# Projecting q and k to DRAM beside the kernel transforms, and attention by groups of key blocks with the output projection woven in

## The chip, the cores and the metric

One core of one Trainium2 chip runs the kernel; the other cores are idle. The metric is the device time of one execution in microseconds. A profile (a trace of one execution) counts from its own zero, and its span is about 2 us shorter than the time. Runs are called fast or slow by whether they lie within 1.5% of the fastest of the same kernel; only fast runs are compared.

Names used below: PE is the matmul array, DVE the vector engine, ACT the scalar engine, POOL and SP the two engines that here mostly issue DMA. Each engine works through its own queue in order. The clock of PE is given as the share of full speed that the profile shows as granted; the DMA share is the mean busy share of the 16 DMA engines.

## The reference, cut to what matters

Two branches share one input x (which is also the q of the first), with S = 2048 positions and D = 640 channels, and are mixed by a gate.

```python
def A(q, k, v, shift_k, ssm_k, ssm_D):          # long convolution
    kv = causal_conv4(k, shift_k) * v           # "shift and multiply"
    y  = irfft(rfft(pad(kv)) * rfft(pad(ssm_k)))[:S] + kv * ssm_D
    return q * y

def B(x, wqkv, wo):                             # local dilated attention
    q, k, v = (x @ wqkv) split into 32 heads of 20
    each position sees 8 keys: itself, -2, -4, ... -14 (masked at the start)
    return softmax(q k^T * 20**-0.5) v  @ wo

g = sigmoid(sum(x * gate_w))
return g * A(x, k, v, ...) + (1 - g) * B(x, ...)
```

The kernel computes the Fourier transforms as matmuls against constants (F1b, then G; back through M, then T). In its names `H` is the transform of ssm_k (from `h_lin`, to which D is added), `Up` that of kv, `Cm` the half-inverted product.

## The kernel before

Positions are laid out by parity, so that the dilated window becomes eight neighbours, in 17 blocks of 121 queries and 128 keys, in groups of 4, 4, 3, 3 and 3 blocks. Scores of two heads are two row-tiled matmuls of 31 rows (20 features and 11 mask features). The parts that matter:

```python
# q/k projection: 50 steps of five 128-row matmuls; each head's 20 rows go to SBUF sets by DMA
frag = (dst[r:r + fb - fa, 0:w], stg[fa - f0:fb - f0, 0:w]);  nc.sync.dma_start(*frag)

# attention, by 8 tiles of four heads (all five groups of blocks inside each): 80 halves
for s in range(len(halves)):
    scores(s + 1)                      # PE scores, then one ACT exp per half
    if 6 <= s < 36: advance(qk, 1)     # the last 30 q/k steps woven in
    if s == 20:     load_h()           # h_lin, 8 loads
    if s == 37:     add_D(); hg = h_early()
    if hg is not None and s % 5 != 4: advance(hg, 1)   # kernel transforms woven in
    advance(kvg, 1)                    # DVE's shift-and-multiply chain
    pv(s)

# FFT of kv with the output projection woven in
while advance(fft, 1):
    k += 1
    if k >= 2:  advance(opg, 1)
    if k == 60: load qg (4 DMAs of 640 KB), load bl (4 of 640 KB)       # 32 rows each
T = p2.tile([128, 64, 2, 32], BF, name="T", tag="Am", bufs=2)
nc.sync.dma_start(T[:], cf["T"]...)

# last inverse step: 6 blocks of up to three positions
    for q in range(4):
        nc.vector.tensor_tensor(rq, yv, rq, ALU.mult)                   # yv is in PSUM
    nc.vector.tensor_tensor(reg, reg, bl[:, t0:t0 + m, :], ALU.add)
    for g in range(4):
        (nc.sync, nc.scalar)[g % 2].dma_start(out..., reg...)
```

The softmax here doesn't subtract the row's maximum and nothing guards it: scores larger than these inputs give would overflow.

## Time and profile before

The median of two runs is 356.44 us (355.08 to 357.79); the profiled span is 354.1 us.

| | before |
|---|---|
| PE, DVE, ACT busy share | 72%, 60%, 47% |
| mean granted PE clock | 0.784 |
| DMA moved | 46.37 MB |

No engine is full over the whole span, so the reading has to go by stages, which the prediction does.

### The profile page before, as it was taken

How to read it: one execution, taken by the hardware profiler on the slowest of the kernel's cores; microseconds unless marked ns; L12 is line 12 of the kernel's file. 1: busy time of each engine (PE TensorE's matmuls, PEld its weight loads, DVE VectorE, ACT ScalarE, POOL GpSimd, SP SyncE). 2: the span in 40 equal slices, each digit the busy share in tenths (PEclk: the TensorE clock that was granted, in tenths of full speed). 3: DMA queues.
4: the chain of work that ended last, by engine and by line, in shares of the span. 5: the costliest groups of instructions: out<-in, count | busy, mean ns of one | idle time of the engine just before them, and what ended most of it. 6: DMA issues, size and time to landing. Idle time of an engine off the chain costs nothing. (4 is left out here: it accounts for less than half of the span.)

```text
span 354.1 us, 9846 instructions
## 1 busy us (share of the span) xinstructions
PE 254.6 (72%) x4355; PEld 174.0 (49%) x4355; DVE 211.4 (60%) x295; ACT 165.9 (47%) x239; POOL 41.2 (12%) x67
## 2 busy tenths in 40 slices
PE   2760599958779999857877888898989488660430
PEld 2330355524336655545655655575657477660320
DVE  1400999692836565857776633844574668671595
ACT  3250264525526555634545585756565577531000
POOL 8910023010150000000000000112111000000000
PEclk9995599999659999755555556999999968867555
DMA  7375854974441499761891019217121507999165
GB/s 200 137 241 178 267 151 118 211 199 102 103 84 31 88 168 163 193 191 30 181 213 51 4 27 217 65 41 170 39 54 38 138 4 164 213 213 212 57 149 132
DMA packets 34603, 46.37 MB, mean 131 GB/s; under 512 B 23757, under 2 KB 28572, under 8 KB 33152
## 3 DMA queue, kind: packets, MB, share of 16 engines
q1 hardware_dynamic: 31088, 35.77, 42.9%
q0 software_dynamic: 2896, 8.66, 9.3%
q10 hardware_dynamic: 576, 1.31, 1.6%
q8 instruction: 34, 0.56, 0.7%
q14 instruction: 9, 0.07, 0.1%
HBM read 27.19 MB, written 7.87 MB: 99 GB/s over the span
## 5 line engine op out<-in xcount | busy, mean ns | idle before, releaser
L421 ACT ACTIVATE ET<-sc 128x726 bf16<-128x726 f32 (+1 forms) x80 | 67.1, 858 | 57.8 <-PE sc L418 57.2
L352 PE MATMUL pj<-xT,W 128*128 128x484 bf16 (+3 forms) x250 | 55.9, 368 | 6.2 <-ACT stg L128 4.0
L274 DVE TENSOR_TENSOR pr<-kh,wl 128x2560 bf16<-128x2560 bf16 x16 | 23.0, 1487 | 28.2 <-DMA kh<-in_A_k_dram 23.4
L485 PE MATMUL s<-Am,G 64*128 64x64 bf16 x1280 | 29.2, 206 | 13.9 <-DVE Hs L130 4.1
L352 PEld LDWEIGHTS <-W 128*128 128x128 bf16 x250 | 21.7, 102 | 29.8 <-issue 11.9
L418 PE MATMUL sc<-qb,kb 31*128 31x121 bf16 x544 | 36.0, 260 | 0.6 <-issue 0.6
L485 PEld LDWEIGHTS <-G 64*128 64x128 bf16 x1280 | 26.1, 105 | 17.9 <-issue 12.1
L435 PEld LDWEIGHTS <-ET 128*128 128x128 bf16 x544 | 22.4, 102 | 20.8 <-ACT ET L421 9.3
L618 PE MATMUL op<-wo,oT 128*128 128x128 bf16 (+1 forms) x170 | 27.3, 310 | 4.3 <-ACT oT L128 3.5
L130 DVE CAST stg<-pj 128x484 bf16<-128x484 f32 (+3 forms) x30 | 17.9, 598 | 20.8 <-PE pj L352 16.2
L130 DVE CAST Am<-s 128x512 bf16<-128x512 f32 x36 | 23.4, 686 | 11.5 <-PE s L468 9.9
L309 PE MATMUL psv<-W,xT 128*128 128x128 bf16 (+1 forms) x170 | 27.6, 327 | 2.8 <-DMA W<-in_B_wqkv_dram 2.8
L525 PE MATMUL i<-M,Hw 128*128 128x128 bf16 x160 | 25.6, 253 | 4.9 <-DVE Hw L513 2.6
L525 PE MATMUL i<-M,Hs 128*128 128x128 bf16 x160 | 26.0, 253 | 4.1 <-DVE Hs L512 4.1
L626 POOL DMA_DIRECT2D b_scr<-fin x18 | 9.6, 531 | 161.7 <-DVE fin L624 137.9
L128 ACT CAST Am<-s 128x512 bf16<-128x512 f32 x44 | 23.6, 610 | 6.7 <-PE s L468 4.6
L525 PEld LDWEIGHTS <-Hs 128*128 128x128 bf16 x160 | 22.5, 154 | 7.0 <-DVE Hs L512 4.5
L130 DVE CAST Hs<-s 128x1024 bf16<-128x1024 f32 x15 | 18.4, 1224 | 11.7 <-PE s L485 11.7
L301 PE MATMUL trx<-ident,xS 128*128 128x128 bf16 x80 | 7.9, 265 | 22.6 <-DMA xS<-in_A_q_dram 20.4
L525 PEld LDWEIGHTS <-Hw 128*128 128x128 bf16 x160 | 22.4, 155 | 3.0 <-DVE Hw L513 3.0
L128 ACT CAST Cm<-i 128x1024 bf16<-128x1024 f32 x15 | 15.2, 1012 | 15.9 <-PE i L525 15.7
L309 PEld LDWEIGHTS <-xT 128*128 128x128 bf16 x170 | 14.7, 106 | 15.4 <-issue 7.2
(73 smaller groups left out, 362.5 us busy)
## 6 DMA issues: line engine op xcount, KB each, us to landing
Hw<-Hs SPq DMA_DIRECT2D x10, 512.0 KB
xS<-in_A_q_dram SPq DMA_DIRECT2D x4, 640.0 KB
kv_scr<-pr POOLq DMA_DIRECT2D x4, 640.0 KB, 5.4
h_lin<-in_A_ssm_k_dram SPq DMA_DIRECT2D x8, 320.0 KB
kv<-kv_scr SPq DMA_DIRECT2D x4, 640.0 KB
qg<-in_A_q_dram SPq DMA_DIRECT2D x4, 640.0 KB
bl<-b_scr SPq DMA_DIRECT2D x4, 640.0 KB
W<-in_B_wqkv_dram SPq DMA_DIRECT2D x3, 800.0 KB
```

The costliest lines, as they stand in the source:

```text
L128: self.nc.scalar.copy(dst, src)
L130: self.nc.vector.tensor_copy(dst, src)
L274: nc.vector.tensor_tensor(pr[:, j].rearrange("p (n c) -> p n c", n=4), kh[:, 3 - j:7 - j, :], wl[:, j, :].unsqueeze(1).to_broadcast([128, ...
L309: nc.tensor.matmul(ps[:, n0:n1], lhsT=xT[:, dt, BP * b:BP * b + 128], rhs=W[:, dt, 2, n0:n1], start=(dt == 0), stop=(dt == NDT - 1))
L352: nc.tensor.matmul(ps[:, 0:n], lhsT=W[:, dt, which, 128 * ft:128 * ft + 128], rhs=rhs, start=(dt == 0), stop=(dt == NDT - 1))
L418: nc.tensor.matmul(sc[:, hh, BP * bb:BP * bb + BP], lhsT=kb[r:r + DH + NF, 128 * b:128 * b + 128], rhs=qb[r:r + DH + NF, BP * b:BP * b + B ...
L421: nc.scalar.activation(ETs[s % NET][:, :, 0:nw], sc[:, :, 0:nw], ACT.Exp, scale=SCALE)
L435: nc.tensor.matmul(O[:, sl * 21:sl * 21 + 21], lhsT=ET[:, hh, BP * bb:BP * bb + 128], rhs=VWs[t // 4][:, b, 4 * (t % 4) + 2 * hf + hh, :], ...
L485: nc.tensor.matmul(o, lhsT=st["G"][rows, j, r, :], rhs=Am[rows, 2 * j + r, :, :], start=(r == 0), stop=(r == 1), tile_position=(64 * c, 0) ...
L525: nc.tensor.matmul(o, lhsT=src[:, c, :, :, 8 * oc + il].rearrange("p q j -> p (q j)"), rhs=M[:, k, :], start=(k == 0), stop=(k == 1), skip ...
L618: nc.tensor.matmul(opf[:, n0:n1], lhsT=oT[:, ft, :], rhs=wo[:, ft, n0:n1], start=(ft == 0), stop=(ft == NDT - 1))
L626: nc.gpsimd.dma_start(dst, fin[r0:r0 + n, :])
```

## The change

Its intent, as far as the diff tells: free SBUF and the order of work. q and k are projected at once, beside the transforms of the kernel, and written to DRAM; attention goes group by group over all heads and streams its group back; so a group's output projection can be woven into the next group's attention, and the FFT stands alone. The last step moves PSUM to SBUF by ACT, so that DVE multiplies from SBUF.

```diff
+    q_scr = dpool.tile([D, QW], BF, name="q_scr")
+    k_scr = dpool.tile([D, KW], BF, name="k_scr")
...
-                    frag = (dst[r:r + fb - fa, 0:w], stg[fa - f0:fb - f0, 0:w])
-                        nc.sync.dma_start(*frag)
+                nc.gpsimd.dma_start((q_scr if which == 0 else k_scr)[128 * ft:128 * ft + 128, :], stg[:, 0:w])
...
+    load_h(0); load_G(pC); load_h(1)          # h_lin by group: 40 loads for 8
+    for b in range(12, NB): vproj(b); advance(kvg, 1)
+    for g in range(2, NG): load_h(g)
+    for k in range(50):
+        advance(qk, 1)
+        if k < 10: advance(kvg, 1)
+        if k == 9: nc.vector.tensor_tensor(h_lin[:, :, :, 0], h_lin[:, :, :, 0], Dz..., ALU.add)
+        if k >= 10 and k % 5 != 4: advance(hg, 1)
...
+    def load_bg(gi):                          # one group back: 8 loads of 20 rows
+        for h4 in range(4):
+            r = slice(32 * h4, 32 * h4 + DH)
+            nc.sync.dma_start(sk(e)[r, :, 0:nb * 128], raw(k_scr[:], ...))
+            nc.sync.dma_start(sq(e)[r, :, 0:nb * BP], raw(q_scr[:], ...))
...
+    halves = [(gi, t, hf) for gi in range(len(GROUPS)) for t in range(NT) for hf in range(2)]
+    def op_half(b, hf):                       # woven into the next group
+        for ft in range(NDT):
+            nc.tensor.matmul(op[:, 0:320], lhsT=oTs[b % 3][:, ft, :], rhs=wo[:, ft, 320 * hf:320 * hf + 320], ...)
...
-            nc.vector.tensor_tensor(rq, yv, rq, ALU.mult)
+            nc.scalar.copy(yt[:, 0:m, 160 * q:160 * q + 160], ps[:, q, 0:160 * m]...)
+        nc.vector.tensor_tensor(reg, yt[:, 0:m, :], reg, ALU.mult)
```

(Some lines are joined or shortened. T, qg and G are now loaded at the start of the FFT, bl in its fourth group.)

## The prediction

> **What bounds the kernel now.** I read the whole-run busy shares first (PE 72%, DVE 60%, ACT 47%: no engine is full), so I cut the span into stages by a table of windows; the columns are the stretch, its length, the busy time of PE, PE weight loads, DVE, ACT and POOL with counts, the granted PE clock, the DMA share and GB/s.
>
> ```profile
> 54.90:86.00 31.10, 26.97 (x160) 13.43 (x160) 23.84 (x18) 13.22 (x30) 4.70 (x6) 0.95 0.67 156
> 86.00:104.00 18.00, 12.39 (x151) 6.56 (x151) 9.68 (x14) 8.61 (x12) 6.84 (x10) 0.65 0.50 101
> 104.00:142.00 38.00, 38.00 (x482) 22.53 (x479) 22.50 (x52) 22.03 (x26) 0.00 (x0) 0.98 0.62 106
> 142.00:212.00 70.00, 53.90 (x1098) 39.62 (x1098) 45.96 (x85) 36.93 (x45) 0.00 (x0) 0.53 0.45 111
> 212.00:277.00 65.00, 56.58 (x927) 39.49 (x924) 36.51 (x48) 39.48 (x57) 9.55 (x18) 0.95 0.39 95
> 305.50:330.00 24.50, 7.49 (x182) 6.96 (x173) 11.34 (x22) 6.87 (x7) 0.00 (x0) 0.73 0.92 206
> 330.00:354.00 24.00, 7.22 (x512) 4.94 (x512) 18.60 (x30) 0.00 (x0) 0.00 (x0) 0.50 0.45 112
> ```
>
> Stages: V projection (0 to 54.9), q/k projection (to 86), attention (to 212: with the rest of q/k it is PE-bound at full clock, 38.00 of 38; with the kernel transforms it is a chain at half clock), FFT with the output projection (to about 277, PE-bound), bare FFT (to 320), the last inverse step. The chain that ended last then shows the end:
>
> ```profile
> 295.13 10.32 DMA qg<-in_A_q_dram
> 305.45 0.02 issue
> 305.47 0.02 SPq L660
> 305.48 0.04 issue
> 305.52 24.38 DMA T<-cf_T
> ```
>
> T is issued at 305.5 behind 5.2 MB of qg and bl and lands at 329.9. But the last eviction of Cm ends at 320.0 (ACT timeline: 317.03 plus 3.02), so only 10 of these 24 us are exposed. After T, DVE alone paces the end:
>
> ```profile
> 315.26 4.83 DVE L663 TENSOR_SCALAR qg<-qg,g_nat 128x640 bf16<-128x640 bf16 x16 [2.10 <-DMA qg<-in_A_q_dram]
> 331.22 2.35 DVE L680 TENSOR_TENSOR qg<-i,qg 128x480 bf16<-128x480 f32 x4 [11.12 <-PE i L673]
> 333.60 1.16 DVE L681 TENSOR_TENSOR qg<-qg,bl 128x1920 bf16<-128x1920 bf16 x1
> ```
>
> **What the Trainium skill says.** (1) "TensorE: Matmul & The Clock Gate", Part 1: the array runs at half clock until it has been busy for about 3.4 us. The trace agrees on the two levels: 0.98 in 104 to 142, 0.50 in nearly every slice of 150 to 216, though PE was some 75% busy there with short matmuls. (2) "SBUF — State Buffer", Door 1: DMA bandwidth goes by the SBUF ports that the partitions reach; 32 rows reach 8 of 16 (189 GB/s at 1 MiB there). The trace agrees: qg and bl, 32 rows per transfer, moved at 206 GB/s (row 305.50), while 3.4 us with the 128-row G in them moved 429 GB/s. By its formula rows 0 to 19 of a strip reach 5 ports (136 GB/s at its 27.2 each) and rows 20 to 30 reach 3 (82): my estimates, which no run before shows. (3) "VectorE: DVE Perf Modes", tier table: tensor_tensor does bf16 from SBUF at 2x, a PSUM operand at 1x. Agrees: 480 elements from PSUM take 648 ns, 1920 from SBUF 1158.
>
> **The change part by part.**
>
> Start. The loads and V projection keep their order: 54.9 as before. Five V blocks now follow at once (6.8 us in the timeline: 64.45 to 71.24): 61.8. Ten q/k steps at 1.0 us: 72.5.
>
> A new wait. The first kernel transform is queued behind step ten and reads h_lin after its D addition, which DVE runs in order after the whole shift-and-multiply chain. Before, that chain began its last quarter at 75.80, so by its rows (0.65 copy, 4 x 1.45, a write wait of 1.2, 2.82, 1.49, 1.49) it would end about 89, plus 0.89 for the addition: 90 to 91. So PE stands from about 73 to 91, **18 us**, which before was filled with q/k and attention. The 40 h_lin loads start at 50.4 (they wait for the transposes out of xS) and G goes between them; 2.6 MB of 128-byte rows took some 14 to 17 us before, so they are in by about 80: not the last wait.
>
> Projection and transforms. Left at 91: 31 wide q/k steps at 1.05, 8 narrow at 0.28, and 32 transform steps at 0.45 (stage 1, 8 matmuls) or 0.55 (stage 2, 32): 34.8 + 16 = 51 us of PE at full clock. Copies are 56 us in ACT's durations, shared by two engines, so hidden. Add 2.5 for a cold clock and 2.5 for the turns from stage 1 to 2: q/k ends near 147. The last 8 transform steps (7 us) lie beside what follows: last k copy 0.6, DRAM write 5 (kv_scr, 640 KB, lands in 5.4), then reading the first group back in 8 pieces of 20 rows, 1.27 MB at about 136 GB/s plus 2: the first two head strips at 160, all at **164.5**.
>
> Attention. 32 exps of 977 ns and 48 of 778: 68.6 us is ACT's floor. PE per half at full clock is 0.63 (4 blocks) or 0.52 (3), read from the 104 to 142 stretch by taking q/k out of its 1.71 and 1.54 us periods. The woven output projection adds 0.68 for five 320-column matmuls (5 x 0.135) or 0.28 for transposes. DVE has 53 us of work in it: not the bound. Group 0: ACT-bound, 16 x 0.98 = 15 left, to 179.5. Group 1 needs, behind the first load, wo (0.8 MB, 3 us), the mask rows (0.7 MB at 82 GB/s, 8.7) and its own 1.27 MB (9.4 + 2): **185.5, a 6 us stall**. Group 1: 8 halves at 1.31 and 8 at 0.98 = 18.4, plus 3 to warm the clock: 207. Group 2: 8 x 1.2 + 8 x 0.8 = 15.8; groups 3 and 4: 15.1 + 2 each for the clock that falls when their nine projection steps are used up: 257. The last group's projection has nothing beside it: three blocks at half to full clock, 8.5: **265.5**.
>
> FFT. No projection in it, so no longer PE-bound; the product steps (Up times Hs) began at 285.94, 297.00 and 308.53 where no projection was left: 11.3 us a group. First product 7.3 after the start plus 2 for Hw, which waits behind T (issued only when the last projection matmul has freed its place); four more groups 45.2; last product to last Cm copy 11.5 (308.5 to 320.0): 66. Ends **331.5**.
>
> End. T and bl are there: the 10 us go. i2 1.3 us, four ACT copies 2.1, then DVE does 1.16 + 1.16 per block of three instead of 2.35 + 1.16: 5 x 2.26 + 1.0 = 12.3 against 18.8; stores 4.1. Total 20: span **351.5**; with the 2.3 by which the time exceeded the span, 354.
>
> So: the end saves 10 + 6 - 2 = 14, and all before it costs about 11 (331.5 against 320). My working is built from waits added one after another; some overlap (the 6 us stall hides the warm-up of the clock, parts of the loads overlap on different ports). I take 6 off: **348 us**.
>
> **The rivals.**
> (a) The reorganisation gains cleanly: no stall at group 1, full clock in attention and FFT. For it: the 38-us stretch held 0.98 with PE full, and dense 320-column matmuls are spread through groups 1 to 4. Against it: the clock fell in 91 to 104 and all of 145 to 216. It would take 6 + 7 + 5 off my walk: 335.
> (b) The clock stays at 0.5 through attention: groups 1 to 4 are then PE-bound at 0.84 + 1.33 per projection half; 26, 23, 20, 20 us instead of 73: +16 us, 368. For it: 142 to 212 never warmed at 77% busy. Against it: PE would be full, and 213 to 218, with projection matmuls, did warm.
> (c) The wait for h_lin is shorter because contention or order differs, say 8 us: 342. Against: DVE is in order, and the rows of the chain are fixed. Or longer: the h_lin and G loads slow the k and v loads of the last quarters: 355.
> (d) The narrow reads (20 of 128 rows) are slower than 136 GB/s: at 80, each load of a group takes 16 us instead of 9, about the length of a group: 365.
>
> **Range and chances.** Central 348; (a) and a short (c) pull to 335, the plain walk is 354, (b) and (d) push to 366. Eight in ten: 334 to 364. Faster by over 2% means under 349.3, slower over 363.6: 0.50, 0.37, 0.13.
>
> **What would show it.** PE idle of 15 to 20 us ended by the h_lin addition, near 73 to 91. First score matmul near 160, attention with a wait on DMA of strm1 at group 1; mean of exps unchanged at 778 and 977. PE clock 0.5 in group 0, mostly above 0.8 from group 1 on. T off the chain; products 11 to 12 us apart; the DVE row of the PSUM multiply replaced by one of about 1.16 us. I am wrong if PE goes through h_lin without standing, if the first score comes before 150, if the exps run without gaps for all 80 halves, or if the FFT takes 80.

## More of the kernel before

The view of slices shows two things at a glance; each digit is one fortieth of the span (8.85 us), in tenths of the full clock and of the DMA engines' time:

```profile
PEclk9995599999659999755555556999999968867555
DMA  7375854974441499761891019217121507999165
```

The clock is at half for seven slices in the middle (attention with the kernel transforms) and at full where dense projection matmuls are present. DMA is full for a slice or two in several places, and for longest near 300 to 330 us.

## The result

The changed kernel takes 414.57 us (median of two runs, 414.27 to 414.87). The ratio is 1.163, with a 95% interval of 1.144 to 1.182. It is slower, and outside the range. Ratios here and below are the mean time of one kernel's fast runs over that of the other's of the same rounds, so they are not quite the ratio of the medians quoted.

The view of slices of the changed kernel (one fortieth is 10.3 us):

```profile
PEclk9995999755799998555555655555585867887555
DMA  7475498999312121978964409501049944690234
```

The DMA row now has a full stretch early (slices 6 to 10, about 50 to 100 us), and the half clock covers attention (168 to 304 us) but for two slices, longer than before. The table of windows, cut where the trace shows the stages begin and end (columns as in the prediction: stretch, length, busy PE, PE weight loads, DVE, ACT and POOL with counts, then granted clock, DMA share, GB/s):

```profile
0.00:71.50 71.50, 44.75 (x381) 27.25 (x385) 30.04 (x22) 27.69 (x41) 17.92 (x30) 0.90 0.69 194
71.50:102.40 30.90, 0.02 (x1) 0.03 (x1) 20.23 (x13) 0.56 (x1) 7.24 (x11) 0.58 0.99 212
102.40:158.00 55.60, 55.46 (x839) 27.70 (x841) 26.30 (x37) 30.01 (x49) 3.74 (x7) 0.95 0.24 77
158.00:178.30 20.30, 6.98 (x186) 5.57 (x187) 5.40 (x7) 6.12 (x10) 1.26 (x10) 0.60 0.65 132
178.30:190.30 12.00, 11.31 (x210) 8.54 (x210) 4.50 (x12) 12.00 (x14) 0.00 (x0) 0.50 0.67 94
190.30:200.60 10.30, 1.76 (x29) 1.26 (x28) 0.75 (x2) 2.12 (x3) 0.00 (x0) 0.50 1.05 197
200.60:294.80 94.20, 90.97 (x1043) 51.58 (x1043) 42.58 (x106) 50.26 (x63) 8.01 (x15) 0.52 0.43 93
...
304.40:379.90 75.50, 50.88 (x1121) 47.39 (x1121) 48.85 (x56) 42.55 (x61) 0.53 (x1) 0.75 0.70 159
379.90:413.10 33.20, 6.25 (x512) 4.72 (x511) 12.56 (x12) 10.61 (x24) 0.00 (x0) 0.56 0.32 81
```

Row by row: PE stands still for 30.9 us beside full DMA; q/k and transforms are PE-bound at full clock, as foreseen; the first group waits for its strips; the first group runs at ACT's pace; a stall; groups 1 to 4 are PE-bound (90.97 of 94.20) at a clock of 0.52; the FFT; the end, in which no engine is busy for more than 13 of 33 us. Set against the prediction's walk, which summed to 351.5 before 6 us were taken off:

| stage | predicted us | measured us | difference |
|---|---|---|---|
| to the last q/k step before transforms | 72.5 | 71.5 | -1.0 |
| PE stands, D's addition | 18.5 | 30.9 | +12.4 |
| q/k with transforms | 56 | 55.6 | -0.4 |
| first group's strips | 17.5 | 20.3 | +2.8 |
| group 0 | 15 | 12.0 | -3.0 |
| stall before group 1 | 6 | 10.3 | +4.3 |
| groups 1 to 4 | 71.5 | 94.2 | +22.7 |
| last projection | 8.5 | 9.6 | +1.1 |
| FFT | 66 | 75.5 | +9.5 |
| end | 20 | 33.2 | +13.2 |
| sum | 351.5 | 413.1 | +61.6 |

The stand: DVE's timeline, then PE's (start, duration, instruction, and in brackets the idle time before it with what ended it):

```profile
92.17 1.49 DVE L255 TENSOR_TENSOR pr<-pr,vn 128x2560 bf16<-128x2560 bf16 x1
101.44 0.89 DVE L473 TENSOR_TENSOR h_lin<-h_lin,Dz 128x160 bf16<-128x160 bf16 x1 [7.78 <-DMA strm<-ca_mk]
```

```profile
102.38 0.79 PE L356 MATMUL s<-F1b,h_lin 64*128 64x128 bf16 x8 [30.90 <-DVE h_lin L473]
```

DVE's chain ended at 93.7, then DVE waited on. The profile names a mask load as the last to land; the program's addition waits for all 40 h_lin loads, the last of which was issued at 95.1, just ahead of it; the last 128-byte packet in the trace ended at 100.4.

The end: ACT's timeline, then DVE's. Between ACT's copies of one block and of the next stand two stores that it issues itself:

```profile
391.09 0.85 ACTq L701 DMA_DIRECT2D out_dram<-qg x2
392.04 1.95 ACT L697 CAST yt<-i 128x480 bf16<-128x480 f32 x4 [3.36 <-DVE qg L699]
```

```profile
394.01 1.16 DVE L698 TENSOR_TENSOR qg<-yt,qg 128x1920 bf16<-128x1920 bf16 x1 [2.96 <-ACT yt L697]
395.21 1.16 DVE L699 TENSOR_TENSOR qg<-qg,bl 128x1920 bf16<-128x1920 bf16 x1
```

The stores wait for DVE's addition, the copies stand behind the stores, and DVE's next multiply waits for the copies: 5.3 us a block, where the instructions alone need 2.3. The row of DVE's PSUM multiply is gone, as planned.

### The profile page after: what moved, and what is told of

It is laid out like the page before. It is cut to its first block, busy times and chain, and to the rows that moved or that the text cites. A ratio compares the mean times of both kernels' runs of the same rounds, so it can differ in the third digit from the quotient of the medians.

```text
span 413.1 us, 9835 instructions
## 1 busy us (share of the span) xinstructions
PE 276.8 (67%) x4351; PEld 179.1 (43%) x4355; DVE 196.0 (47%) x276; ACT 181.9 (44%) x264; POOL 39.8 (10%) x76
## 4 chain that ended last, share of the span: by engine, by line
PE 32%; issue 23%; SPq 15%; DMA 12%; DVE 8%; ACT 7%; ACTq 1%; POOL 1%; POOLq 0%; DVEq 0%
SPq L439 10%; PE pj L326 9%; PE i L424 7%; DMA xS<-in_A_q_dram 5%; PE op L590 5%; PE s L373 4%; SPq L214 3%; DMA b_scr<-fin 3%; DMA Hw<-H 3%; ACT yt L697 2%; ACT Up L128 2%; PE sc L547 2%; DVE qg L698 2%; DVE qg L699 2%; PE s L356 1%
## 5 line engine op out<-in xcount | busy, mean ns | idle before, releaser
L547 PE MATMUL sc<-strm 31*128 31x121 bf16 x544 | 42.1, 293 | 19.1 <-DMA strm<-q_scr 18.4
L590 PE MATMUL op<-wo,oT 128*128 128x320 bf16 x170 | 47.9, 445 | 1.9 <-DVE fin L596 1.0
L128 ACT CAST Am<-s 128x512 bf16<-128x512 f32 x59 | 31.4, 617 | 28.9 <-PE s L356 14.1
L596 DVE TENSOR_SCALAR fin<-op,omg 121x320 bf16<-121x320 f32 x34 | 18.7, 551 | 42.8 <-PE op L590 39.1
L547 PEld LDWEIGHTS <-strm 31*128 31x128 bf16 x544 | 22.6, 120 | 37.3 <-issue 24.1
L424 PE MATMUL i<-M,H 128*128 128x128 bf16 x160 | 29.6, 278 | 10.7 <-DVE H L411 5.4
L128 ACT CAST stg<-pj 128x484 bf16<-128x484 f32 (+3 forms) x33 | 16.2, 498 | 36.3 <-DMA q_scr<-stg 17.8
L356 PE MATMUL s<-F1b,h_lin 64*128 64x128 bf16 x160 | 8.6, 227 | 32.5 <-DVE h_lin L473 30.9
L424 PEld LDWEIGHTS <-H 128*128 128x128 bf16 x160 | 24.1, 159 | 12.0 <-DVE H L411 6.1
L373 PEld LDWEIGHTS <-G 64*128 64x128 bf16 x1280 | 23.0, 100 | 13.5 <-issue 13.1
L567 PE MATMUL O<-VW,ET 128*128 128x21 bf16 x544 | 28.4, 183 | 0.3 <-ACT ET L550 0.3
L573 DVE RECIPROCAL rd<-O 121x12 f32<-121x12 f32 (+1 forms) x40 | 9.7, 242 | 37.8 <-PE O L567 35.6
L567 PEld LDWEIGHTS <-ET 128*128 128x128 bf16 x544 | 20.6, 105 | 14.9 <-issue 14.1
L590 PEld LDWEIGHTS <-oT 128*128 128x128 bf16 x170 | 19.7, 129 | 14.0 <-issue 1.8
```

The costliest lines, as they stand in the source:

```text
L128: self.nc.scalar.copy(dst, src)
L373: nc.tensor.matmul(o, lhsT=st["G"][rows, j, r, :], rhs=Am[rows, 2 * j + r, :, :], start=(r == 0), stop=(r == 1), tile_position=(64 * c, 0) ...
L424: nc.tensor.matmul(o, lhsT=src[:, c, :, :, 8 * oc + il].rearrange("p q j -> p (q j)"), rhs=M[:, k, :], start=(k == 0), stop=(k == 1), skip ...
L547: nc.tensor.matmul(sc[:, hh, BP * bb:BP * bb + BP], lhsT=kb[r:r + DH + NF, t, 128 * bb:128 * bb + 128], rhs=qb[r:r + DH + NF, t, BP * bb:B ...
L567: nc.tensor.matmul(O[:, sl * 21:sl * 21 + 21], lhsT=ET[:, hh, BP * bb:BP * bb + 128], rhs=VW[:, b, 4 * t + 2 * hf + hh, :], start=True, st ...
L590: nc.tensor.matmul(op[:, 0:320], lhsT=oTs[b % 3][:, ft, :], rhs=wo[:, ft, 320 * hf:320 * hf + 320], start=(ft == 0), stop=(ft == NDT - 1))
```

## The experiments

All outputs are right. The kernel before had medians of 354 to 357 us in their rounds. The changed kernel itself was timed only twice, in a round of its own, so a difference of 4 us from it (e2, e4) is not clear of the intervals; three variants of it that gained nothing came to 413.8, 415.4 and 414.8 us (e5, e8, e10), which speaks for its 414.6. Theories at the start: (1) the end is ACT's queue order; (2) the stand is the order on DVE; (3) the clock in attention depends on how much dense matmul work there is; (4) narrow reads are limited by the rows they reach. The rival to (2) is that DMA itself is the bound there, and the rival to (3) that the clock follows busy time alone.

### The end: stores out of ACT's queue (e1)

```diff
-            (nc.sync, nc.scalar)[g % 2].dma_start(raw(outf, ...
+            nc.sync.dma_start(raw(outf, ...
```

> The changed kernel with all 24 output stores issued from SP instead of half of them from ACT. Theory A: at the end ACT, whose queue holds the stores between its copies, waits for DVE's addition before it may start the next copies, so a block of three takes 5.3 us instead of about 2.3. Then the end (379.9 to 413.1, 33.2 us) becomes about 20 us, the time falls by 12 to 14 us to about 401, and nothing before 380 changes. Rival B: the stores themselves (2.6 MB in 32-row transfers) or the copies' speed set the period: the end stays at 30 us or more, the time falls by less than 3 us.

Measured: 404.67 us over four runs, one of them slow; 404.12 over the three fast ones (ratio 1.133 against 1.163). In its profile (slow, so only the order is read), DVE's timeline, DVE goes without a wait through the blocks:

```profile
387.79 1.16 DVE L698 TENSOR_TENSOR qg<-yt,qg 128x1920 bf16<-128x1920 bf16 x1 [6.56 <-ACT yt L697]
388.99 1.16 DVE L699 TENSOR_TENSOR qg<-qg,bl 128x1920 bf16<-128x1920 bf16 x1
390.06 1.15 DVE L698 TENSOR_TENSOR qg<-yt,qg 128x1920 bf16<-128x1920 bf16 x1
```

The first three blocks follow each other in 2.27 us; later ones wait 0.65 and 1.59 us for copies again. Theory A holds, with 10 us for the 12 to 14 expected. It is the cheapest repair of the change: one line.

### The stand before the first transform (e3, e2, e7, e7b, e9)

e3 puts the addition for the first two groups ahead of the end of DVE's chain:

```diff
+        if b == 15: add_D(0)      # in the V loop, ahead of a chain step
         advance(kvg, 1)
+        if b == 15: add_D(1)
-        if k == 9: nc.vector.tensor_tensor(h_lin[:, :, :, 0], ...)
```

(Left out: the other three parts stand ahead of their groups' transforms, and the run also sends the copies of q and k to ACT at first.)

> The changed kernel with the addition of D split into the five groups, and those of the first two groups put ahead of the end of DVE's shift-and-multiply chain. Theory A: the 31 us in which PE stands before the first transform (71.5 to 102.4) come from DVE's order (chain, then one addition that needs all 40 loads); the stand shrinks to under 10 us and the time falls by 20 to 28 us, to about 390. Rival B: DMA is full there (0.92 to 1.12 share), so the work left over only moves: PE stops less here, but the chain, pushed back by the waiting for the loads, or the weight and h_lin loads hold it up later, and the time falls by less than 12 us.

Measured: 420.72 us (ratio 1.182), slower by 6 us than the changed kernel. The first transform did start at 72.5, but the profile has two new lines, from DVE's and from ACT's timeline:

```profile
84.65 0.30 DVE L394 TENSOR_TENSOR h_lin<-h_lin,Dz 128x32 bf16<-128x32 bf16 x1 [15.44 <-DMA h_lin<-in_A_ssm_k_dram]
```

```profile
99.41 0.56 ACT L128 CAST stg<-pj 128x484 bf16<-128x484 f32 x1 [27.32 <-DMA q_scr<-stg]
```

DVE stood 15.44 us for the second group's loads, with its chain behind it; and ACT could not refill a q buffer until q's first store had landed, a store that was issued only at 93.4, because in POOL's queue it stands behind a kv write that waits for the chain. PE stopped again, from 75.5 to 101. My theory A falls: the order on DVE was one of three waits, and taking it away alone brings up the next.

e2 only splits the addition and leaves every part behind the chain:

```diff
     def h_gen():
         for g in range(NG):
+            add_D(g)
```

> The changed kernel with the addition of D split into five, each put just ahead of its group's transform, all still behind DVE's whole shift-and-multiply chain. In the changed kernel the chain ended at 93.7 and the one addition waited on to 101.4 for the last of the 40 h_lin loads. Theory A: those 7.8 us are the loads; the first transform then starts near 94.6 instead of 102.4 and the time falls by 6 to 8 us, to about 407. Rival B: DVE's chain alone, or a store or load after it, sets the pace: PE only stands later, for a later group's loads or for the q store, and the time falls by less than 3 us.

Measured: 410.58 us (ratio 1.158), 4 us less than the changed kernel. The first transform starts as expected, with DVE's chain as the last wait (PE's timeline):

```profile
94.60 0.79 PE L356 MATMUL s<-F1b,h_lin 64*128 64x128 bf16 x8 [22.39 <-DVE h_lin L394]
```

So 7.8 of the 30.9 us were the wait for loads that the first group does not need. By the medians a little over half of it reached the end; the intervals overlap (1.150 to 1.167 against 1.144 to 1.182).

e7 gives PE more work to do ahead of the addition, and takes q's and k's stores out of POOL's queue; e7b is the same kernel again for a profile.

```diff
-                nc.gpsimd.dma_start((q_scr if which == 0 else k_scr)...
+                nc.scalar.dma_start((q_scr if which == 0 else k_scr)...
-        if k == 9:      # D's addition
+        if k == 24:
-        if k >= 10 and k % 5 != 4: advance(hg, 1)
+        if k >= 25 and k % 5 != 4: advance(hg, 2)
```

> The changed kernel with what PE may do before D's addition made longer: transforms are woven in from q/k step 25 instead of 10 (two at a step), the addition stands at step 24, copies of q/k go to ACT until then, and the stores of q and k are issued from ACT, so that they do not stand behind the kv writes in the POOL queue (which is what held PE from 75.5 to 101 when D's addition alone was taken away). Theory A: the stand was a matter of order, PE has 25 steps of 1.03 us to do from 62.5 (to about 88 if the stores keep up, to 98 if each takes its 8 to 10 us), and the stand shrinks from 31 to 5 to 15 us: the time falls by 12 to 18 us, to about 400. Rival B: with DMA full from 50 to 100 the q/k stores only push the h_lin and kv transfers back, so the addition comes later by as much as PE did ahead: the time falls by less than 6 us.

> The run with the transforms woven in from q/k step 25 once more, for a profile in the fast state (its own profile fell into a state with a clock of 0.54; three untimed-by-profile runs took 409 to 415 us). Theory A': the stand moved rather than went: the addition still waits for the last h_lin load near 101, PE has run out of q/k work near 88 and the stores hold it, and what was gained of the stand is given back between 100 and 200. Rival B': the stand is gone as in the slow profile (12 us left of 31) and the time is lost in later stages, by chance or by the clock. Told apart by the time of the last q/k matmul, 158 in the changed kernel: near 155 for A', 145 for B'.

Measured: e7 411.92 us over its three fast runs (409.5 to 415.4, ratio 1.165; 413.67 with the slow one); e7b 408.86 us, a single run. The profile of e7b, DVE's and PE's timelines:

```profile
107.73 0.90 DVE L473 TENSOR_TENSOR h_lin<-h_lin,Dz 128x160 bf16<-128x160 bf16 x1 [7.26 <-DMA strm<-ca_mk]
```

```profile
108.68 1.21 PE L356 MATMUL s<-F1b,h_lin 64*128 64x128 bf16 x16 [17.00 <-DVE h_lin L473]
```

The stand is 17 us for 30.9 (and PE waited 4.8 us at 74 to 79 for ACT's copies, which waited for q's first store), but the addition comes 6.3 us later than in the changed kernel, because the h_lin loads do: SP issued the last of them by 104 instead of 95.6. The last q/k matmul starts at 155.2 instead of 157.8. That is A' and the rival of e7: q's and k's stores, sent earlier, pushed h_lin's transfers back by nearly as much as PE had got ahead.

This suggests that DMA is the bound from 50 to 100 us. In the changed kernel 11.20 MB moved between 50 and 101 us, at a share near 1.0 but only 220 GB/s, in 23,232 packets of which 21,696 had under 512 bytes; h_lin alone is 20,480 pieces of 128 bytes. The Trainium skill's page "DMA: Bandwidth & Descriptors", section "Why small descriptors are slow (HBM only)", says that each packet and each descriptor carries a fixed overhead, which weighs most on short ones; the trace agrees in direction, since from 20 to 25 us, where most packets had 512 bytes and more (43 of 702 had fewer), DMA moved 321 GB/s. The direct test moves 2 MB out of the way (e9):

```diff
     load_h(0)
-    load_G(pC)
     load_h(1)
     for b in range(12, NB): ...
     for g in range(2, NG):
         load_h(g)
+    load_G(pC)
```

> The changed kernel with the load of G (2 MB, first read by the fifth transform step) put behind the last h_lin load instead of ahead of the second. Theory A: from 50 to 100 us DMA is the bound, so 2 MB less ahead of h_lin (10 us at the 204 to 230 GB/s of this stretch) let the last h_lin land and the chain's write wait end earlier: the addition comes near 94 to 96 instead of 101.4, and the time falls by 4 to 7 us if G is then not the next wait. Rival B: h_lin's 128-byte pieces are issued at a pace of their own (1.1 us each on SP), whatever lies beside them: the addition stays within 2 us of 101 and so does the time.

Measured: 412.20 us (ratio 1.162, so no gain that the interval of 1.153 to 1.172 would show), although the stage itself did what A expects: the addition came at 94.06 and the first transform at 95.0, 7.4 us earlier. By the FFT's first product the lead was 4.7 us (312.1 for 316.8), by its last 2.2 (366.3 for 368.6). The last 128-byte packet ended at 93.3 instead of 100.4, although G costs SP only 0.5 us to issue, and DVE's chain ended at 91.2 instead of 93.7: what else moves on DMA is shown to hold h_lin and the chain back. What the stage gains is partly given back later.

### The clock in attention (e4, e4t)

Both add five matmuls that nobody reads to each half of the projection: 192 columns, 128 rows in e4, 31 rows in e4t.

```diff
+        for ft in range(NDT):        # e4t: rows 0:31 of both operands
+            nc.tensor.matmul(op[:, 320:512], lhsT=oTs[b % 3][:, ft, :], rhs=wo[:, ft, 0:192], ...)
```

> The changed kernel with five idle matmuls of 128 rows and 192 columns added to every half of the output projection, into columns of the same PSUM tile that nobody reads (5 x 192 = 960 columns, some 0.4 us at full clock, 0.8 at half, 34 times). Theory A: the clock of 0.50 in groups 1 to 4 is a matter of too little dense matmul work, as the stretch of before with 484 and 512 columns in each half held 0.98; with more of it the mean clock of 200 to 295 rises above 0.7 and this stretch gets shorter than 94 us, by 5 us or more. Rival B: the clock isn't set by that; it stays at 0.50 to 0.55 and the stretch gets longer by about 34 x 0.8 = 27 us, the time about 440.

> The same as the run with idle matmuls, of the same columns and number, but with 31 rows instead of 128. Told apart: if PE time alone keeps the clock up, this run does what the 128-row one does. If the filled rows of the array count, the clock stays near 0.50 here and rises there. If neither rises, both are longer by about 27 us (near 440) and the amount of idle work is not what decides.

Measured: e4 410.48 us (two runs, ratio 1.153), 4 us less by the medians in spite of the added work, though the intervals overlap; e4t 431.47 us (ratio 1.212). The windows over groups 1 to 4, first of e4, then of e4t:

```profile
200.30:291.60 91.30, 85.12 (x1179) 58.91 (x1178) 42.53 (x108) 49.61 (x63) 7.98 (x15) 0.80 0.42 95
```

```profile
200.30:308.00 107.70, 104.09 (x1177) 61.34 (x1174) 41.56 (x109) 49.86 (x63) 7.98 (x15) 0.53 0.36 80
```

With the same number of matmuls and columns, the clock was 0.80 with 128 rows and 0.53 with 31. PE was busier in the second (97% against 93%), so busy time alone is not what keeps the clock up; between these two runs only the filled rows differ. The same count and columns took 16.4 us less at the higher clock. The first group of lines of e4 and of the changed kernel (PE matmul groups between 200 and 300 us: count, busy us, mean ns) shows what the clock is worth:

```profile
L590 PE MATMUL op<-wo,oT 128*128 128x320 bf16 x160 | 34.2, 356 | 3.9 <-DVE fin L599 3.1 <-DVE oT L583 0.6
```

```profile
L590 PE MATMUL op<-wo,oT 128*128 128x320 bf16 x151 | 44.5, 459 | 1.8 <-DVE fin L596 1.0 <-DVE oT L583 0.6
```

A projection matmul of the same shape takes 356 ns on average instead of 459. The clock in e4 still fell to 0.50 twice inside groups 1 to 4, for 10 us (225.5 to 235.7) and 20 us (266.5 to 286.9), so the amount added is near the edge. What share of filled rows would hold it throughout was not tried.

### The narrow reads of the first group (e5)

```diff
-            nc.sync.dma_start(sq(e)[r, :, 0:nb * BP],
+            (nc.gpsimd if gi == 0 else nc.sync).dma_start(sq(e)[r, :, 0:nb * BP],
```

> The changed kernel with the four q loads of the first group issued from POOL's queue, beside the four k loads on SP's. Theory A: these reads of 20 rows are limited by the rows they reach and by what moves at all, not by SP's queue: the last strip's q still lands about 14 us after the first issue (177.7 less 163.6), group 0 starts within 2 us of before and the time stays within 3 us of 414. Rival B: one queue issues and moves them one after another; two queues bring all in some 4 to 6 us earlier and the time falls by that.

Measured: 413.82 us (ratio 1.164), no change. The four strips still came one after another; the last score wait ended at 176.1 with the first load issued at 161.2 (14.9 us; 14.1 in the changed kernel). By the criteria set beforehand this is theory A, but the test is weak: k's loads were issued only from 165.7, and counted from the last q/k matmul group 0 began 16.8 us after it instead of 20.2. That the rows reached are the limit is not shown. The changed kernel's trace shows something else: in the 14.1 us from 163.6 to 177.7 DMA moved 1.96 MB at 139 GB/s, and by the packets' sizes only 1.27 MB of it is strips; 479 packets of 1280 bytes (0.61 MB) are rows of wo, whose load was issued at 167.2, while the strips were still on their way. From 165 to 168, before wo's packets, DMA moved 152 GB/s. The Trainium skill's page "DMA: Bandwidth & Descriptors", section "Issuing engines are not separate DMA queues", says that loads issued from several engines run on the same 16 DMA engines, so that spreading them saves only issue time; this run agrees.

### The loads beside the FFT (e8, b1, b2, b4, b5, b7, e10)

e8 moves the load of qg out of the FFT's start in the changed kernel (after the inverse of its second group).

> The changed kernel with the load of q for the end (2.6 MB, 32 rows a transfer) issued after the second group's inverse instead of at the start of the FFT. Theory A: between 309 and 330 DMA is full of it (0.98 to 1.08), and PE stands three times with no release that the profile shows (0.4, 1.9 and 3.5 us), while packets of the instruction queue land only now and then: these stands and the late Hw go, the FFT takes 68 to 71 us instead of 75.5, and the time falls by 4 to 7 us, less if the same comes back where the load now lies. Rival B: the stands are not DMA's; PE stands as often, and the time stays within 2 us.

Measured: 415.40 us (ratio 1.169). Theory A is not borne out in time: PE stood 7.4 us in the FFT with no visible release, as against 7.6 in the changed kernel, and the Up copies again waited 5.65 us for a projection store at the start.

b1 asks the same of the kernel before: is the 10 us wait for T to be had by loading earlier?

```diff
-        if k == 60:
+        if k == 42:
+            T = p3.tile([128, 64, 2, 32], BF, name="T");  load T
             load qg
+        if k == 60:
             load bl
-    T = p2.tile([128, 64, 2, 32], BF, name="T", tag="Am", bufs=2);  load T
```

> The kernel before with T in a place of its own, and T and q loaded some 40 us earlier than before, bl as before. Theory A, of the prediction: about 10 us of the last chain of before is the wait for T, so the last inverse step starts near 321 instead of 331 and the time falls by 9 to 10 us, to about 346 (ratio 0.973). Rival B: the earlier loads delay the swaps of H beside which they run, or the addition then waits for bl (2.6 MB issued at 301): the time falls by less than 5 us.

Measured: 357.35 us (ratio 1.010), slower. T and qg were ready, but the swap of H was issued 10.6 us later than before, and PE stood (SP's and PE's timelines):

```profile
284.34 0.47 SPq L503 DMA_DIRECT2D Hw<-Hs  x1
```

```profile
295.74 1.62 PE L485 MATMUL s<-Am,G 64*128 64x64 bf16 x53 [7.03 <-issue]
```

"issue" is time in which the engine waited for nothing that the profile shows. b4 therefore sends qg behind the swap (at k == 46) and T at k == 30.

> The kernel before with T in its own place, loaded in a quiet stretch (near 260), and q loaded right behind the fourth swap (near 282) instead of ahead of it; bl as before. When both stood ahead of that swap in SP's queue, the swap was issued 10.6 us later (284.3 for 273.7), PE stood 7.0 us with no release that the profile shows, and the 10 us from T were lost again before they came. Theory A: it was the order in SP's queue; now the fourth product is on time and the end starts near 322: the time falls by 8 to 10 us, to about 346. Rival B: DMA full beside the FFT holds PE back wherever the load is put: PE again stands several us without a visible release, and the gain is under 5 us.

Measured: 355.11 us (ratio 0.999). T did not go to a quieter place: SP, with nothing else to do, issued it right behind the third group's swap in both runs (b1, then b4):

```profile
241.88 2.13 SPq L650 DMA_DIRECT2D T<-cf_T  x1
```

```profile
240.81 2.13 SPq L650 DMA_DIRECT2D T<-cf_T  x1
```

There it held up a store of the projection, whose SBUF DVE's next eviction reuses; PE ran out of work (DVE's timeline of b4, then the windows of b4 and of the kernel before):

```profile
252.80 0.88 DVE L624 TENSOR_SCALAR fin<-op,omg 121x640 bf16<-121x640 f32 x1 [6.52 <-DMA b_scr<-fin]
```

```profile
248.00:254.00 6.00, 2.21 (x76) 1.68 (x74) 1.20 (x2) 2.23 (x3) 0.02 (x1) 1.00 0.41 148
```

```profile
248.00:254.00 6.00, 5.81 (x158) 4.08 (x157) 3.38 (x4) 3.51 (x5) 1.07 (x2) 1.00 0.14 35
```

So the second group's product began at 265.5 instead of 260.0, and of the 9.2 us by which the fourth was late (306.2 for 297.0), some 5.4 came from here. In b1 the same wait was 6.4 us. The swap was now at 279.3, and PE stood 4.6 us once more. The same 4 us in the kernel before and in b4 (columns as above):

```profile
288.00:292.00 4.00, 3.65 (x42) 3.65 (x43) 2.57 (x3) 2.98 (x5) 0.00 (x0) 0.69 0.02 4
```

```profile
288.00:292.00 4.00, 0.37 (x26) 0.37 (x28) 0.37 (x1) 0.00 (x0) 0.00 (x0) 1.00 1.08 229
```

DMA is idle in one and full in the other, and PE is busy 3.65 us in one and 0.37 in the other. So the 10 us at the end of the kernel before were not simply there for the taking: in both places tried, T and qg cost nearly as much as they had at the end. A place for T clear of the projection's stores was not tried.

b2 and b5 add to b1 and b4 the change's own last step, with ACT copies and all stores from SP.

```diff
-            nc.vector.tensor_tensor(rq, yv, rq, ALU.mult)
+            nc.scalar.copy(yt[...], ps[...]);  one tensor_tensor from yt
-            (nc.sync, nc.scalar)[g % 2].dma_start(raw(outf, ...
+            nc.sync.dma_start(raw(outf, ...
```

> The kernel before with T and q early (as in the run before this), with the change's ACT copies out of PSUM in the last step, and all output stores issued from SP. Theory A: a block of three then costs DVE 2.3 us instead of 3.5, and ACT is held by nothing: 4 to 6 us less than with T early alone, some 14 to 15 in all, to about 342 (ratio 0.96). Rival B: copies and stores set the period as they do in the changed kernel: no gain over T early alone, or a loss.

> The same loads as in the run before this, with the ACT copies out of PSUM in the last step and all output stores from SP. Those two were worth 2.5 to 3.6 us beside the earlier order of loads (DVE's last stretch 14.0 us for 17.9, less the wait for the first copies). Theory A: they add to the gain: 3 to 4 us below the run before this, to about 342. Rival B: the end is then bound by the stores, and nothing is added.

Measured: b2 354.84 us (ratio 1.002, b1 1.010), b5 354.06 us (ratio 0.995, b4 0.999). The step is worth some 2.5 us on b1 by the medians; on b4 the intervals overlap.

b7 is b5 with qg and bl loaded in packets of 1280 bytes:

```diff
-                nc.sync.dma_start(qg[32 * g:32 * g + 32], raw(x2, 16 * g * D, [[64 * D, 32], [1, 16 * D]]))
+                for o in range(2):
+                    nc.sync.dma_start(qg[32 * g:32 * g + 32, o::2, :],
+                                      raw(x2, (16 * g + o) * D, [[64 * D, 32], [2 * D, 8], [1, D]]))
```

> The kernel before with T and q early, ACT copies and stores from SP (the last of the runs before), but the loads of q and bl broken up: every second position by one transfer, so that a packet has 1280 bytes instead of some 15 to 20 KB (0.84 MB in 57 packets between 288 and 292 us, while PE stood 4.6 us there with no release that the profile shows, and the one packet of the instruction queue landed in just that window). Theory A: PE's instructions come by the same 16 DMA engines and wait behind long data packets; with short ones the stands of 4.5 and 2.1 us in the FFT shrink to under 2 us together, the fourth product comes near 290 instead of 296, and the time falls to 345 to 349. Rival B: it isn't the packets' length but the mere load, or something else: the stands stay, the time stays at 353 to 355, or rises because short packets move slower.

Measured: 352.60 us, ratio 0.988 (0.979 to 0.996): faster than both kernels, by a little over 1% (unclear by the rule of 2%). The stands fell from 6.6 to 4.0 us in all, not to under 2. e10 does only this to the changed kernel.

> The changed kernel with q and bl for the last step loaded in 1280-byte packets and nothing else. When this came with three other fixes the four together gave 24 us, some 6 more than the three had given one by one. Theory A: those 6 are the short packets: PE's stands without a visible release in the FFT (7.2 us in the changed kernel's profile) fall to half or less, the FFT from 75.5 to about 70, the time by 3 to 6 us. Rival B: the packets' length does not matter here, the stands stay and the time is within 2 us of 414.5; the 6 us came from the fixes helping each other.

Measured: 414.79 us (ratio 1.171), and the stands were 9.5 us instead of 7.6. So packets' length does not explain them, and b7's gain is not shown to come from it. PE's stands were mostly, but not only, beside full DMA: the kernel before stood 2.3 us, from 280.65 to 282.97, at a DMA share of 0.02. One thing holds for all of them. In the FFT of twelve kept traces (the kernel before, the changed one, e2, e6, e8, e9, e10, b1, b2, b4, b5, b7) PE stands for 1 us or more with no visible release 31 times, and each time the stand ends 1.28 to 1.62 us after the end of a 16 KB packet of the instruction queue (in b1 the packet ended at 294.32, the stand at 295.74). So PE was most likely waiting for its next instructions. No run tests it; why the packet is late, even with DMA idle, stays open.

### All repairs at once (e6)

e6 is the changed kernel with the edits of e1, e2, e4 and e10.

> The changed kernel with what helped, all at once: D's addition split by group (4 us by its run), the idle dense matmuls in the projection (4 us), the output stores from SP only (10 us), and the loads of q and bl in 1280-byte packets (0 to 6 us by the theory of the run beside this). If the costs lie in different stretches, as the traces say, they add: 414.5 less 18 to 24, some 391 to 397. Rival: one of them hides another, and it stays above 399. In either case it stays well slower than the kernel before, since the stand of 20 us before the first transform, the clock of 0.5 in the first group, the 10 us stall at the second and the FFT without other work remain.

Measured: 388.52 us over its three fast runs (387.2 to 392.7, ratio 1.095; 390.62 with the slow one), 26 us less than the changed kernel. The four edits alone gave about 10, 4, 4 and 0 us, so they add, and some 8 us more came than their sum. In e6's profile groups 1 to 4 took 85.6 us at a clock of 0.86, for 91.3 at 0.80 in e4 with the same attention code, which is most of it; why the clock held longer is not shown. It stays 9.5% above the kernel before.

## Why the prediction was wrong

By its own steps:

- **Start and q/k with transforms**: right. 71.5 for 72.5, and 55.6 us for 56, at a clock of 0.95.
- **"A new wait"**: the mechanism was right, the size was not: 30.9 us for 18. The failing sentence is the one that has h_lin "in by about 80: not the last wait". I took h_lin's time from the kernel before, where it moved nearly alone (2.62 of the 2.92 MB between 124.5 and 142 us). Here it shared full DMA with kv, k, v, G and q. The last load held the addition to 101.4 (e2, e9), and the chain itself, with a write wait of 8.4 us where I had put 1.2, ended at 93.7 instead of 89.
- **First group's strips**: 20.3 us for 17.5. The trace doesn't speak against the rate of 136 GB/s: DMA moved 152 GB/s while the strips were alone (165 to 168). The step that failed puts wo and the mask rows "behind the first load". Wo's packets ran among the strips, which got 1.27 of the 1.96 MB moved in 14.1 us (90 of 139 GB/s). The stall before group 1 was 10.3 us for 6: from the first issue of its strips (183.7) to the last score wait (200.6) 2.68 MB moved at 158 GB/s, 1.13 MB of it in the long packets of kv's load, for which the working has no term. A second queue did not change the time (e5).
- **"Attention"**: this is the largest miss, 22.7 us in groups 1 to 4. I had the clock at full there but for short warm-ups, because the 38 us of before with woven projection had held 0.98. Rival (b) of the prediction, with the clock at 0.5, was what happened; its own sum of 16 us was still short of it. The step that fails is the reading of the 38-us stretch: it held the clock with five matmuls of 484 or 512 columns and 128 rows in nearly every half, about 1.02 of 1.54 to 1.71 us. Here five of 320 columns stand in about every second half, the scores between them fill 31 rows, and that is not enough: e4 raised the clock by adding dense columns, and e4t showed that the same columns with 31 rows do not; between the two lie 16.4 us.
- **"FFT"**: 75.5 us for 66. The first product came 12.4 us after the start (7.3 plus 2 foreseen), with Up's copies waiting 5.46 us for a projection store whose SBUF they reuse; later groups took 13.1, 15.1, 12.6 and 11.1 us for 11.3 each. Some 7.6 us are PE's stands with no visible release, those of 1 us or more each ended shortly after an instruction packet; the working has no term for them, and moving the load only moved them (e8).
- **"End"**: 33.2 us for 20. T is off the chain, as predicted, and the multiply from SBUF takes 1.16 us, as predicted. I had not seen that ACT's queue also holds stores, which wait for DVE. e1 gives 10 us of it back.
- **The 6 us taken off** for overlaps were in the wrong direction. The stand, the strips and the stall were all longer than estimated, and in all three transfers ran beside others that the working had placed elsewhere or left out.

The gain that was expected at the end, 14 us, is thus smaller than it looked even without the ACT queue: in the kernel before the wait for T was not turned into time by the two orders of loads tried (b1, b4).

## What to carry to other kernels

A duration of a transfer or a clock from one stage holds in another only if what runs beside it is the same: before re-using it, add up the bytes and the packets of the new stage, and the filled rows of its matmuls. When an engine gets new work in a loop, list everything that is already in its queue there, stores too, and ask what each of them waits for. A wait at the end of a chain is worth its length only if the transfer has a place where it holds up nothing that another engine waits for, stores included.

## What the Trainium skill lacked or had wrong

- "TensorE: Matmul & The Clock Gate", Part 1, ties the clock to how busy the array has been. Here PE was busy 90.97 of 94.20 us at a clock of 0.52 (changed kernel) and 104.09 of 107.70 at 0.53 (e4t), while 85.12 of 91.30 with more 128-row columns gave 0.80 (e4). The page does not say that the filled rows count.
- "SBUF — State Buffer", Door 1, gives no figure for several loads of 20 rows at once. Eight of them moved 152 GB/s while they ran alone (165 to 168 us) and got 90 of 139 GB/s beside wo's load.
- "DMA: Bandwidth & Descriptors" has no trn2 figure for 128-byte pieces from HBM beside other traffic: here 11.20 MB, with 21,696 of 23,232 packets under 512 bytes, took 51 us at 220 GB/s with DMA full.
- "Runtime: NRT & Kernel Launch", on instruction fetch, has no figure for what a late block of instructions costs PE. Here PE stood up to 7.03 us (b1), 4.56 (b4) and 3.53 (changed kernel), each time until 1.28 to 1.62 us after an instruction packet ended. That the one causes the other is not shown by a test.
